# First batch's pairs loaded in rows of 8 tokens per partition, their factors handed over by TensorE with selection matrices; x casts first in a block

## The chip, the cores and the metric

The kernel runs on one core of a Trainium2 chip. Time is device microseconds for one execution. A time quoted for a kernel is the median of several runs; a profile shows one execution in detail, and its span leaves out about two microseconds that lie around it.

The engines are named as the profile names them: PE is TensorE's matmul stream (PEld its weight loads), DVE is VectorE, ACT is ScalarE, POOL is GpSimd, SP is SyncE, which here only issues DMAs. ACT and POOL issue DMAs too.

## The reference, cut to what matters

Two stages. The first is a state-space scan over 4 batches, 8 heads, 768 tokens, head width 32, state width 16, in chunks of 32 tokens:

```python
cum = np.cumsum(np.log(a), axis=-1)                 # within a chunk
L = np.exp(cum[:, :, :, None] - cum[:, :, None, :]) * causal
y_intra = einsum('bhij,bhjd->bhid', (C @ B.T) * L, x)
y_inter = einsum('bhin,bhnd->bhid', C, state) * exp(cum)
state = exp(sum(la)) * state + sum_j(B_j x_j * exp(cum_last - cum_j))
y = y_intra + y_inter
```

The second is a gated feed-forward layer over the 3072 tokens, with the heads laid side by side (256 columns) and a hidden width of 1536:

```python
out = (np.maximum(y @ w_gate, 0) * (y @ w_val)) @ w_out
```

The decay between two tokens is a ratio of running products of `a`. So the kernel multiplies each row of C by the running product at its token (the factor FC) and each row of B by its inverse (FB); the scan then becomes plain matmuls with a causal mask.

## The kernel before, in words

**Tiling.** Work goes in chunks of 128 tokens. Two chunks are a pair (256 tokens); a batch has PPB = 3 pairs, the program 12. A feed-forward block is 512 tokens, two pairs; there are 6 blocks. The 12 slices of 128 hidden columns are counted by f.

**Layout of B and C.** `load_rows` (L75) loads a whole batch of B or C in one DMA: partition q*32 + r holds, for heads q and q + 4 (index t), the 24 consecutive tokens from 24 r on (K = 24), 16 values each. In this layout each partition has a contiguous stretch of tokens, which `factors` (L161) needs for the running product: a scan over 24 tokens in each partition, a 32x32 transpose, a scan over the 32 partitions' totals, a transpose back, a product. The result is FC, [128, 2 per batch, 24].

`scale` (L194) multiplies rows by factors and writes bf16; `turn` (L203) transposes 32x32 blocks of 32-bit words on VectorE, after which the state index lies on the partitions; `tidy_b`, `tidy_c` (L209, L221) put the tokens in order, as BT and CT (CT twice, each with one head of a partition group masked out by `tmask`).

**A pair's attention.** `cast_x` (L239) makes x bf16. `rows_b` (L250) transposes BT on TensorE and copies it (tile bt). `G` (L260) forms the products of C and B into four PSUM banks; `gevac` (L278) brings them to SBUF, two banks through ACT with the causal mask applied by POOL (`causal`), two through DVE with a mask product. `astep` (L298) adds bt times x to the state in PSUM (A_ps), `sevac` (L307) copies it out (Sm); `state` is both. `inter` and `Dm` (L322, L334) form y from the state and from the masked products, `yevac` (L348) copies it to yT.

**The feed-forward part.** `gvh` (L374) does half a block (256 tokens) of one f: gate and val matmuls, Relu on ACT, product on DVE; `gv` (L360) does 512 tokens. `fout` (L390) multiplies by w_out; `foevac` evacuates and stores through SP.

**What sets the order.** Every engine runs its instructions in the order in which the program issues them (`in_order`, L16, adds this as a dependency). There is no planner: the loop over blocks names, for each f, what is interleaved there. In block b the pairs are P = 2b + 2 and Q = 2b + 3, prepared for the next block; W = 2b + 1 is finished in the middle of block b. `scale_new` (L464) scales the next batch, `turn_new` turns it.

**Queues.** SP issues loads of a, B, C, x and the stores; ACT issues the second piece of `a` and the first C; POOL issues the weights (`weights(f0, f1)`, L141, for slices f0 to f1 of gate and val; `weights_out`, L147), which are cast to bf16 on the way. `wait_for` (L154) is a one-element POOL copy that holds POOL's later DMA issues back until a load has landed. `keep_warm` (L130) issues filler matmuls. Shared PSUM tiles (`bank`, L69) rotate over six banks.

**Start.** Lines L416 to L446: factors of batch 0, its C and B scaled, turned and tidied on DVE and ACT, pair 0's attention, the beginning of pair 1's. Then the loop over blocks, whose block 0 finishes pair 1 (gevac(1) at f = 0, L475; state, inter, Dm from L484).

## Time and profile before

| | |
|---|---|
| median of 7 runs | 137.55 us (135.96 to 140.48) |
| the profiled execution | 136.55 us, of it span 134.5 us |
| mean granted TensorE clock | 0.975 |
| PE busy | 119.4 us, 89% of the span |
| DVE busy | 93.4 us, 69% |
| ACT busy | 80.8 us, 60% |
| POOL busy | 44.4 us, 33% |
| DMA | 12.07 MB in 34,701 packets, 26,496 of them under 512 B |

Issue to landing, medians: x loads (128 KB each) 4.9 us; B 3.8 and C 4.3 (384 KB each); gate and val weights (256 KB written each) 5.0 and 5.6; w_out (768 KB written) 10.3.

How to read it: busy shares are averages over stages that have different limits. The chain of waits says, for each moment, which work the end of the program hung on; the busy times by window say which engine had no time left in a stage. Blocks start (first gvh matmul) at 14.1, 37.4, 57.4, 78.2, 96.5 and 114.6 us from the span's start.

### The profile page before, as it was taken

The numbers are of one execution on the slowest core, as the hardware profiler recorded it, in microseconds if no ns is written. First come the engines' busy times: TensorE is split into PE (matmuls) and PEld (weight loads), VectorE is DVE, ScalarE is ACT, GpSimd is POOL, SyncE is SP. The second block draws the span as 40 slices with busy tenths as digits, with TensorE's granted clock in tenths as the row PEclk, the third lists the DMA queues.
The fourth block names the chain that finished last, engine by engine and source line by source line (L and its number), as shares of the span: only waits on it lengthen the run. The fifth ranks groups of instructions, "written<-read, shape, count | busy, mean of one in ns | idle before, by whom it ended". The sixth has DMA issues, their size and how long they took to land.

```text
span 134.5 us, 2889 instructions
## 1 busy us (share of the span) xinstructions
PE 119.4 (89%) x1057; PEld 77.0 (57%) x1057; DVE 93.4 (69%) x210; ACT 80.8 (60%) x177; POOL 44.4 (33%) x75
## 2 busy tenths in 40 slices
PE   6829849799999789999499999999999999999990
PEld 2204526347786347786147786467784477854770
DVE  6676476998588867668556879775686965687510
ACT  4055647564598743598554498954889635876410
POOL 3417355655250951251950270402524012200000
PEclk9975799999999999999999999999999999999999
DMA  2994899990239700239600227200270002200021
GB/s 56 279 173 66 142 222 251 212 190 4 83 92 292 86 0 5 78 113 279 83 0 0 78 80 123 38 2 0 83 156 0 0 5 78 78 5 0 0 101 55
DMA packets 34701, 12.07 MB, mean 90 GB/s; under 512 B 26496, under 2 KB 34688, under 8 KB 34688
## 3 DMA queue, kind: packets, MB, share of 16 engines
q1 hardware_dynamic: 30800, 8.87, 31.2%
q0 software_dynamic: 3184, 2.36, 11.6%
q10 hardware_dynamic: 704, 0.67, 1.5%
q8 instruction: 8, 0.13, 0.4%
q14 instruction: 5, 0.04, 0.1%
HBM read 11.11 MB, written 3.15 MB: 106 GB/s over the span
## 4 chain that ended last, share of the span: by engine, by line
PE 68%; DVE 9%; DMA 7%; issue 5%; POOL 4%; ACT 3%; SPq 1%; ACTq 0%; DVEq 0%; POOLq 0%
PE o L395 22%; PE gv L383 13%; PE gate L365 12%; PE val L368 11%; DMA xr<-in_x_dram 3%; DMA cr<-in_C_dram 3%; DVE h L372 3%; PE g L267 3%; PE y L340 3%; POOL sqB L198 2%; PE A_ps L303 2%; PE y L329 2%; DVE h L387 1%; PE bb L255 1%; POOL gs L274 1%
## 5 line engine op out<-in xcount | busy, mean ns | idle before, releaser
L372 DVE TENSOR_TENSOR h<-r,val 128x512 bf16<-128x512 bf16 x48 | 32.2, 683 | 8.5 <-ACT r L371 7.8
L371 ACT ACTIVATE r<-gate 128x512 bf16<-128x512 f32 x48 | 28.3, 598 | 13.2 <-PE gate L365 10.0
L395 PE MATMUL o<-wo,h 128*128 128x256 bf16 x288 | 34.9, 273 | 0.1
L395 PEld LDWEIGHTS <-h 128*128 128x128 bf16 x288 | 27.4, 98 | 5.2 <-issue 1.3
L365 PE MATMUL gate<-yT,wg 128*128 128x512 bf16 x96 | 28.6, 379 | 0.0
L368 PE MATMUL val<-yT,wv 128*128 128x512 bf16 x96 | 28.6, 379 | 0.0
L274 POOL TENSOR_SCALAR_AFFINE_SELECT gs<-gs 128x512 bf16<-128x512 bf16 (+1 forms) x24 | 12.2, 530 | 44.0 <-ACT gs L285 44.0
L387 DVE TENSOR_TENSOR h<-r,gv 128x256 bf16<-128x256 bf16 x48 | 19.8, 421 | 7.3 <-ACT r L386 6.7
L291 DVE TENSOR_TENSOR gs<-g,maskUT 128x512 bf16<-128x512 f32 x24 | 15.5, 686 | 12.0 <-PE g L267 8.9
L386 ACT ACTIVATE r<-gv 128x256 bf16<-128x256 f32 x48 | 18.4, 386 | 3.3 <-PE gv L383 1.8
L383 PE MATMUL gv<-yT,wg 128*128 128x256 bf16 x96 | 18.8, 278 | 0.9 <-ACT yT L353 0.5
L383 PE MATMUL gv<-yT,wv 128*128 128x256 bf16 x96 | 18.6, 276 | 0.0
L368 PEld LDWEIGHTS <-wv 128*128 128x128 bf16 x96 | 9.4, 98 | 11.4
L365 PEld LDWEIGHTS <-wg 128*128 128x128 bf16 x96 | 9.0, 98 | 11.4 <-issue 4.2
L353 ACT CAST yT<-y 128x512 bf16<-128x512 f32 x12 | 7.0, 585 | 10.0 <-PE y L340 8.5
L285 ACT CAST gs<-g 128x512 bf16<-128x512 f32 x12 | 7.1, 588 | 8.9 <-PE g L267 8.9
L383 PEld LDWEIGHTS <-wg 128*128 128x128 bf16 x96 | 9.0, 99 | 3.2 <-issue 1.6
L311 DVE TENSOR_TENSOR Sm<-A_ps,smask 128x256 bf16<-128x256 f32 x20 | 8.2, 410 | 3.4 <-PE A_ps L303 3.4
L383 PEld LDWEIGHTS <-wv 128*128 128x128 bf16 x96 | 9.5, 99 | 1.3
L227 POOL TENSOR_SCALAR CT<-tqC,tmask 128x264 bf16<-128x264 bf16 (+1 forms) x10 | 9.3, 932 | 0.0
L225 ACT ACTIVATE CT<-tqC,tmask 128x264 bf16<-128x264 bf16 (+1 forms) x13 | 6.7, 526 | 4.2 <-DVE tqC L205 4.2
L198 POOL TENSOR_TENSOR sqC<-cr,FC 128x384 bf16<-128x384 f32 x6 | 5.3, 879 | 11.8 <-DMA cr<-in_C_dram 9.3
(65 smaller groups left out, 105.8 us busy)
## 6 DMA issues: line engine op xcount, KB each, us to landing
xr<-in_x_dram SPq DMA_DIRECT2D x24, 128.0 KB, 4.9
out_dram<-ob SPq DMA_DIRECT2D x10, 256.0 KB, 2.2
br<-in_B_dram SPq DMA_DIRECT2D x4, 384.0 KB, 3.8
cr<-in_C_dram SPq DMA_DIRECT2D x3, 384.0 KB, 4.3
wg<-in_moe_w_gate_dram POOLq DMA_DIRECT2D x3, 256.0 KB, 5.0
wv<-in_moe_w_val_dram POOLq DMA_DIRECT2D x3, 256.0 KB, 5.6
wo<-in_moe_w_out_dram POOLq DMA_DIRECT2D x1, 768.0 KB, 10.3
cr<-in_C_dram ACTq DMA_DIRECT2D x1, 384.0 KB, 4.5
```

Of the source, the lines that this page charges most:

```text
L227: eng.tensor_scalar_mul(dst, src, tmask[:, t:t + 1])
L274: nc.gpsimd.affine_select(out=dst, in_=dst, pattern=[[0, n], [1, 128]], compare_op=ALU.is_ge, fill=0.0, base=0, channel_multiplier=-1)
L291: nc.vector.tensor_tensor(out=d[:, q], in0=g[q], in1=m, op=ALU.mult)
L311: nc.vector.tensor_tensor(out=n, in0=A_ps, in1=smask, op=ALU.mult)
L365: nc.tensor.matmul(out=g, lhsT=wg[:, k, fs], rhs=yT[:, k, tk], start=(k == 0), stop=(k == 1))
L368: nc.tensor.matmul(out=v, lhsT=wv[:, k, fs], rhs=yT[:, k, tk], start=(k == 0), stop=(k == 1))
L371: nc.scalar.activation(r, g, AF.Relu)
L372: nc.vector.tensor_tensor(out=fst[b][:, f], in0=r, in1=v, op=ALU.mult)
L383: nc.tensor.matmul(out=gv_[:, j], lhsT=w[:, k, fs], rhs=yT[:, k, tk], start=(k == 0), stop=(k == 1), skip_group_check=True)
L386: nc.scalar.activation(r, gv_[:, 0], AF.Relu)
L387: nc.vector.tensor_tensor(out=fst[b][:, f, u * 256:(u + 1) * 256], in0=r, in1=gv_[:, 1], op=ALU.mult)
L395: nc.tensor.matmul(out=o[:, ts % 2], lhsT=fst[b][:, f, ts * 128:(ts + 1) * 128], rhs=wo[:, f], start=(f == 0), stop=(f == NF - 1), skip_gr ...
```

## The change

**Batch 0.** B and C of the first batch are no longer loaded as a whole but pair by pair, in a layout of 8 consecutive tokens per partition (K8 = 8): partition q*32 + r holds tokens 256 p + 8 r on. Each pair's B and C take four DMAs each (one for each group q of 32 partitions, 32 KB); pair 0's alternate between ACT and SP, pair 1's follow, pair 2's go out inside block 0.

The factors are still computed in the layout of 24 tokens per partition. `give` brings them into the other layout: token group r of pair p is the s-th third of partition row c with 3c + s = 32p + r, so three FP32 matmuls with 0/1 selection matrices (`hand`, made by POOL in `hands`), each on a third of FC's columns, add up to the pair's factors in PSUM. `take` forms the inverse and, if asked, copies the factors to SBUF. `scale8`, `turn8`, `tidy8_b`, `tidy8_c` are the counterparts of the old functions on 8 tokens per partition. Pairs 1 and 2 are scaled on POOL.

**Start.** `tmask` is built on POOL instead of DVE, bd and smask later on DVE (`more_masks`). Fillers: 14 become 6, then 5 after `give(1)`; the 3 before Dm(0) become 5.

**Weights.** `weights(4, 8)` before block 0 and `weights(8, NF)` at its f = 1 become one `weights(4, NF)` at f = 0, after gevac(1).

**Loads in the blocks.** Block 0's loads go out at f = 0 behind a POOL memset that follows the weights: pair 2's B and C, x(2), batch 1, x(3), x(4), batch 2. Block b > 0 loads the x of pairs P + 1 and P + 2, and then batch b + 2 instead of b + 1.

**Casts first.** In blocks b > 0 POOL casts P and Q at f = 0 and 1 and scales the next batch at f = 2 to 5; before, scaling came at f = 0 to 3 and the casts at f = 4 and 5.

```diff
+    def load_pair(p, j, q, eng):
+        b, c0 = p // PPB, 2 * (p % PPB)
+        src = {"B": B, "C": C}[j][b].rearrange("(t q) s n -> q t s n", t=2)
+        eng.dma_start(
+            out=st[p]["rows"][j][R * q:R * q + R],
+            in_=src[q][:, c0 * 128:(c0 + 2) * 128].rearrange("t (r k) n -> r t (k n)", r=R))
...
-    nc.sync.dma_start(out=al[:, 0:1, 1:], in_=av[:, 0:1])
-    nc.scalar.dma_start(out=al[:, 1:2, 1:], in_=av[:, 1:2])
+    nc.sync.dma_start(out=al[:, 0:2, 1:], in_=av[:, 0:2])
...
-    rows["C", 0] = load_rows(C, 0, nc.scalar, "cr")
-    rows["B", 0] = load_rows(B, 0, nc.sync, "br")
-    load_x(0, nc.sync)
+    for j in "CB":
+        for q in range(4):
+            load_pair(0, j, q, (nc.scalar, nc.sync)[q % 2])
+    load_x(0, nc.sync, nc.scalar)
+    for j, q in (("C", 0), ("C", 1), ("C", 2), ("C", 3), ("B", 0), ("B", 1), ("B", 2), ("B", 3)):
+        load_pair(1, j, q, nc.scalar if j == "C" and q < 2 else nc.sync)
     load_x(1, nc.sync)
...
+    hand = const.tile([128, PPB, 3, 128], FP32)
+
+    def hands(p0, p1, eng):
+        n = p1 - p0
+        eng.memset(hand[:, p0:p1].rearrange("p c s i -> p (c s i)"), 0.0)
+        for q in range(4):
+            h = hand[R * q:R * q + R, p0:p1, :, R * q:R * q + R]
+            nc.gpsimd.affine_select(
+                out=h, in_=h, pattern=[[R, n], [-1, 3], [1, R]], base=R * p0,
+                channel_multiplier=-3, compare_op=ALU.not_equal, fill=1.0)
...
+    hands(0, 1, nc.gpsimd)
     make_identity(nc, ident)
...
+    hands(1, 2, nc.gpsimd)
...
+    def give(p):
+        s = st[p]
+        f = bank("f8", (128, 2, K8))
+        for i in range(3):
+            nc.tensor.matmul(out=f, lhsT=hand[:, p, i], rhs=FC[:, 0:2, K8 * i:K8 * i + K8],
+                             start=(i == 0), stop=(i == 2))
+        s["f"] = {"C": f}
+        return f
+
+    def take(p, keep):
+        s = st[p]
+        f = s["f"]["C"]
+        s["f"]["B"] = fb = const.tile([128, 2, K8], FP32, name="fb%d" % p)
+        if keep:
+            s["f"]["C"] = fc = const.tile([128, 2, K8], FP32, name="fc%d" % p)
+            nc.vector.tensor_copy(fc, f)
+        nc.vector.reciprocal(fb, f)
+
+    def scale8(p, j, eng):
+        s = st[p]
+        s.setdefault("sq", {})[j] = sq_ = att.tile([128, K8 // 2, 2, N, 2], BF16, tag="sq8" + j, name="sq8")
+        for t in range(2):
+            eng.tensor_tensor(
+                out=sq_[:, :, t],
+                in0=s["rows"][j][:, t].rearrange("p (a k n) -> p a n k", n=N, k=2),
+                in1=s["f"][j][:, t].rearrange("p (a k) -> p a k", k=2)
+                .unsqueeze(2).to_broadcast([128, K8 // 2, N, 2]), op=ALU.mult)
...
     factors(0, 2)
+    give(0)
+    give(1)
+    keep_warm(5)
+    more_masks(0)
+    scale8(0, "C", nc.vector)
+    take(0, False)
+    turn8(0, "C")
+    wait_for(0, st[0]["rows"]["B"][96:97, 0, 0:1])
     weights(0, 4)
+    tidy8_c(0, 0, nc.scalar)
+    scale8(0, "B", nc.vector)
+    turn8(0, "B")
+    tidy8_c(0, 1, nc.scalar)
+    tidy8_b(0, nc.vector)
+    take(1, True)
+    more_masks(1)
     cast_x(0, nc.scalar)
+    scale8(1, "C", nc.gpsimd)
+    scale8(1, "B", nc.gpsimd)
...
     gevac(0, half=False)
+    hands(2, 3, nc.gpsimd)
     sevac(0, 0)
+    turn8(1, "C")
+    turn8(1, "B")
+    tidy8_c(1, 0, nc.scalar)
+    tidy8_b(1, nc.vector)
+    tidy8_c(1, 1, nc.vector)
+    keep_warm(5)
     Dm(0)
...
+        def loads():
...
+            if b == 0:
+                load_batch(1)
+            for n in (P + 1, P + 2):
+                if n < NPAIR:
+                    load_x(n, nc.sync)
+            load_batch(b + 2)
...
             if b == 0 and f == 0:
                 gevac(1)
-            if b > 0:
-                scale_new(f)
+                wait_for(1, st[1]["xr"][0:1, 1, 0, 0:1])
+                weights(4, NF)
+                for k in range(8):
+                    if k == 0:
+                        nc.gpsimd.memset(st[2]["rows"]["C"][:, 0, 0:1], 0.0)
+                    load_pair(2, "CB"[k // 4], k % 4, nc.sync)
+                load_x(2, nc.sync)
+                loads()
+                give(2)
+            if b > 0 and more and f < 2:
+                cast_x(P + f, nc.gpsimd)
+            if b > 0 and f >= 2:
+                scale_new(f - 2)
             if b == 0 and f == 1:
                 cast_x(1, nc.scalar)
-                weights(8, NF)
+                take(2, True)
                 wait_for(2, st[2]["xr"][0:1, 1, 0, 0:1])
                 weights_out(0, NF)
-            if b == 0 and f == 3:
+            if b == 0 and f == 2:
                 state(1, 0)
...
             if b == 0 and f == 4:
-                tidy(P, nc.vector, nc.scalar, nc.gpsimd)
-            if b == 0 and f < 8:
-                scale_new(f - 4)
-            if at("cast P", 5, 4, 4):
-                cast_x(P, nc.gpsimd)
-            if at("cast Q", 8, 5, 4):
-                cast_x(Q, nc.gpsimd)
+                scale8(2, "C", nc.gpsimd)
+                scale8(2, "B", nc.gpsimd)
+            if b == 0 and f == 6:
+                turn8(2, "C")
+                turn8(2, "B")
+                tidy8_c(2, 0, nc.scalar)
+                tidy8_c(2, 1, nc.gpsimd)
+                tidy8_b(2, nc.vector)
+            if b == 0 and 5 <= f < 9:
+                scale_new(f - 5)
+            if b == 0 and f in (4, 8):
+                cast_x(P + (f == 8), nc.gpsimd)
+            if b > 0 and f < 6:
+                scale_new(f - 2)
```

## The prediction

> **What bounds the kernel now.** I read the page's busy line first, then the chain of waits in order of time, then busy time by block, then the DMA queues in short windows.
>
> The chain gives the opening. Its columns are start, length, what (us).
>
> ```profile
> 1.23 4.49 DMA cr<-in_C_dram
> 5.74 1.04 DVE sqC L198 x2
> 6.81 0.58 DVE tqC L205
> 7.39 0.92 DVE sqB L198 x2
> 8.33 0.59 DVE tqB L205
> 8.94 0.39 DVE BT L216
> 9.37 0.39 PE bb L255 x2
> ...
> 11.00 1.22 POOL gs L274 x2
> ```
>
> Nothing starts before the whole batch's C has landed (5.72); then five VectorE steps on 768 tokens run in series up to 9.33. GpSimd's causal masks (to 12.2) and TensorE's y lead to the first feed-forward matmul at 14.1.
>
> Busy time by feed-forward block (blocks 1 to 4, bounds at each block's first gv matmul; columns: stretch, length, then busy us and count for PE, PEld, DVE, ACT, POOL, then clock, DMA share, GB/s):
>
> ```profile
> 37.38:57.35 19.97, 18.54 (x175) 12.37 (x174) 15.20 (x32) 12.88 (x30) 8.23 (x13) 1.00 0.41 93
> 57.35:78.20 20.85, 18.62 (x178) 12.58 (x177) 14.53 (x30) 13.39 (x30) 8.66 (x14) 1.00 0.40 89
> 78.20:96.45 18.25, 18.25 (x177) 12.40 (x175) 13.31 (x27) 13.08 (x29) 4.99 (x9) 1.00 0.28 60
> 96.45:114.55 18.10, 18.10 (x175) 12.26 (x173) 13.34 (x28) 12.55 (x28) 4.84 (x8) 1.00 0.19 44
> ```
>
> Blocks 3 and 4 are TensorE without a gap, 18.1 to 18.25. Blocks 1 and 2 are 1.8 and 2.65 longer. The same chain says why, here in block 2:
>
> ```profile
> 59.68 4.59 DMA xr<-in_x_dram
> 64.33 0.88 POOL sqB L198
> ...
> 66.00 0.89 POOL sqB L198
> 66.89 0.57 POOL xb L242
> 67.50 0.27 PE A_ps L303
> ```
>
> GpSimd works in order: its four scalings of the next batch wait for that batch's load (the waits put 4.6 us on C's landing), the casts of x stand behind them, and TensorE's state matmul behind those (TensorE idle 2.2 us before 67.5, 1.4 us before 47.59). VectorE is the limit once, in block 0, from 22 to 32 (8.81 busy of 9.00 between 22 and 31).
>
> In block 0 the DMA engines are also full from 14 to 30. Queue 0 (GpSimd's casting weight loads) and queue 1 (SP's) between 26 and 27 us; columns packets, MB, share of 16 engines:
>
> ```profile
> q0 software_dynamic: 372, 0.19, 138.7%
> q1 hardware_dynamic: 130, 0.02, 20.9%
> ```
>
> The last weight load before wo lands 8.2 us after its issue at 17.77, wo 10.3 us after 20.09, that is at 30.4, when fout first wants it.
>
> **What the Trainium skill says.** "DMA: Bandwidth & Descriptors", section Queues, rings and completion order: each DMA engine goes round-robin over its queues packet by packet. The two lines above agree: against queue 0's packets of about 500 B (0.19 MB in 372), x's 128 B pieces get 0.02 MB in a microsecond; alone, between 7 and 8, they got 0.15. "TensorE: Matmul & The Clock Gate", What's actually happening: the array runs at half rate until it has been busy for about 3.4 us. Agrees: filler matmuls come every 0.43 us until 5.0, every 0.215 later; and the clock is again 0.50 from 9 to 15, after TensorE idled from 6.3 to 9.4. "FP8 and Floating Point Precision", TensorE Precision Notes: true FP32 takes four passes. No FP32 matmul is in this trace.
>
> **The change part by part.**
>
> *Loads at the start.* One 384 KB load of C and one of B become four 32 KB loads each for pair 0, then eight more for pair 1. Issue costs 0.46 us for 256 rows and 1.05 for an x load of 1,024 pieces, so some 0.35 for 64 rows (estimate on that slope). ACT issues seven DMAs, 6 x 0.35 + 1.0 = 3.1: its table load (1.28) then ends near 5.4 instead of 3.0; first use at 6.25, so free. SP's first B row is out by 2.6 and lands near 4.9 (2.0 to landing for a small load, plus queueing); C by 4.3. C stops being what is waited for; FC is: the scan starts when al lands (2.84 now, 0.1 later as one DMA), FC at 4.2.
>
> *The handing over.* Three FP32 matmuls of 16 columns for each pair, not in the trace. Low: three bf16 issues, 0.3 us. High: four passes, each with a 0.13 us weight load at half clock, 3 x 4 x 0.13 = 1.6. I take 1.0: f at 5.2. VectorE's five bd memsets (0.5) move into this wait and cost nothing; if f came at once they would cost 0.5.
>
> *VectorE on 256 tokens instead of 768.* A scale of 384 is 0.53 to 0.56, so 128 is some 0.26; a turn of 384 is 0.57 and of 32 0.21, so 128 is 0.31. C scale 0.5, reciprocal of 16 0.2 (48 take 0.45), turn 0.3, B scale 0.5, turn 0.3, tidy 0.37: 5.2 + 2.2 = 7.4 against 9.33.
>
> *GpSimd at the start.* The selection matrices: a memset of 384 is 0.41 (0.10 for 1, 0.20 for 128), four selects of 96 0.27 each (0.29 for 128): 1.5 a set. First set by 2.3; identity, tmask, triangle 1.7; second set by 5.5. The weight issue moves from 5.48 to 5.7: covered, weights are wanted at 12.5 and land near 12. **give(1)** waits for that second set on TensorE's in-order queue, and five fillers (2.1 cold) and then rows_b(0) stand behind it: bb at 7.5 to 8.2 instead of 9.37. Third set (1.5) after the first masks: idle there.
>
> *Up to block 0.* New on GpSimd ahead of the masks: four scalings of pair 1, 1.44 (0.36 each from 0.88 for 384), from 7.75 to 9.2; masks end at 10.5 instead of 12.2. VectorE gets two turns (0.6) and take(1) (0.3). Following the old intervals, G(1) ends and the first gv starts at 12.5: **1.6 us earlier**.
>
> *Small moves.* Fillers: 14 become 6 at the start (TensorE then waits for FC anyway), 3 become 5 before Dm(0): 2.1 us cold from 8.6 end at 10.7, where Dm waits for the mask at 10.5; I count 0. give(2) (0.3 to 1.6) and take(2) (0.3) come between f=0 and f=1 of block 0; TensorE idles 1.4 us before 18.93 there, waiting for VectorE, so give(2) lies in that gap, and take(2) is the price, paid back by state(1, 0) one f earlier. The output stores of block 0 stand on SP behind batch 2's two loads (1 us of issue); nothing waits for a store there, three ob buffers cover it.
>
> *Weights 4 to 12 in one pair of DMAs.* Half were issued at 12.3; now all go after gevac(1)'s mask, where the second pair went at 17.06: with the 1.6, at 15.4. Flow starts 1.7 later (12.29 to 14.0 now). Alone queue 0 moves 0.20 MB/us (15 to 17); 1.05 MB with SP's loads joining after 18.8 at about 0.15: done 23.4, landed near **24.0**. val of f=4 wants it at 20.8 (22.4 less 1.6): TensorE waits 3.2. VectorE's factors(2, 8) (2.1) run inside that wait.
>
> *x(2) and GpSimd's queue.* SP now issues eight pair-2 loads (2.8 us) ahead of x(2), all behind a GpSimd memset at 17.3, against weights that win the round-robin. I put x(2)'s landing at **24.5** (19.6 before). GpSimd stands at that wait, and wo, pair 2's scalings, the cast, and batch 1's scalings are behind it: 0.17 + 1.03 + 1.44 + 0.62 + 0.88 + 0.9 + 0.88 + 0.88 = 6.8, so batch 1's C can be turned at 31.3. VectorE, in order, has turn, h, turn, Sm, h left: 0.57 + 0.69 + 0.57 + 0.4 + 0.69 = 2.9. The last h is at 34.2 (31.87 before): **2.3 us later than before**. wo, issued at 24.7, flows some 5 us from 26.5: 32, where fout begins; covered.
>
> *Blocks 1 and 2.* Batches load a block earlier and the P cast comes first, of an x loaded a block earlier. The Q cast waits for an x issued at the block's start (landed +5 us), the scalings end at +9.1; TensorE wants P's state at about +8.5 and VectorE the C turn at +8.7 (three scalings, +8.3). All covered, the turn by 0.4. Gain 1.75 + 2.6 = **4.35**. Blocks 3 to 5 unchanged: TensorE has no gap to give.
>
> Sum on the profiled execution (span 134.5, time 136.55): +2.3 - 4.35 = -2.0, 134.5. The median of the runs is 137.55, 1.0 above it, spread 3.3%; I carry the difference over: **135.5**.
>
> **The rivals.**
>
> A, likeliest (0.50): as summed, -2.0, own range -3.5 to -0.5, so 134.0 to 137.0: x(2)'s landing is known to 1.5 us.
>
> B (0.24): the loads are not late. For it: with less requested by SP, weights run at 0.20 throughout, landing at 22. Then VectorE's 8.5 us (eight h 5.5, turns of pair 2 0.6, of batch 1 1.14, tidy 0.4, Sm 0.8) bound block 0: fout's first group 1.0 early, -1.0 - 4.35: 132.2. Against it: GpSimd still waits for x(2).
>
> C, slower (0.20): x(2) starves behind the weights. For it: queue 1's 0.02 MB between 26 and 27; at that rate x(2) lands only after the weights, the eight pair loads and itself: 24 + 0.7 + 1.8 + 2 = 28.5. Everything behind GpSimd's wait moves with it: 4.0 later, +2.0: 139.6. It breaks even at a landing of 26.5 and is slower by 1% from 27.9. Against it: 18.8 to 24 leaves SP's queue some of the engines (between 22 and 24 it had about half).
>
> D (0.06): the hand-over fails as a short cut: 1.6 us for give and selects at twice my price hold give(1) and its fillers to 9.5, the start gains nothing, and the delay passes to the weights' issue: 1.6 later, -0.4: 137.1. Against it: the select rows.
>
> **How the numbers follow.** About 1% (1.4 us) is what can be told from no change. Faster by over 1%: A 0.33, B 0.24: 0.57. Within: A 0.15, C 0.01, D 0.04: 0.20. Slower: A 0.02, C 0.19, D 0.02: 0.23. The range 131.8 to 139.2 leaves out a third of B below (0.08) and half of C above (0.11).
>
> **What would show it.** C's scale at 5.2 with FC before it, bb near 7.9, first gv at 12.5; TensorE idle at val of f=4 until 24; GpSimd's gate copy of x(2) at 24.5 and VectorE waiting for GpSimd's sqC near 31; no TensorE wait on xb in blocks 1 and 2, each near 18.3. It is wrong if that gate copy comes before 22 or after 26.5, if give takes over 1.6, or if the Q cast's landing now holds the scalings and the turn.

## The result, and the profile after

The changed kernel takes **138.41 us** (median of 12 runs, 137.34 to 143.12) where the kernel before takes 136.91 (31 runs, 135.96 to 140.48): the ratio is **1.0095, interval 1.0057 to 1.0132**. A gain of 2 us was forecast; it lost 1.5. Its profiled execution took 137.93 us with a span of 136.2 us. In what follows a ratio is always to the kernel before, run beside it on the same chip. In some of the runs below the profiled execution, or most of the timed ones, fell into a slower state of the chip: no time is read from such a trace, and no ratio stands where none could be formed.

Busy time by block, first of the kernel before (the opening and block 0), then of the changed one (the opening, then blocks 0 to 3); the columns are those of the prediction's block view, stretch, length, the five engines, clock, DMA share, GB/s.

```profile
0.00:14.11 14.11, 9.63 (x57) 3.51 (x58) 9.39 (x40) 5.65 (x11) 5.70 (x17) 0.80 0.79 138
14.11:37.38 23.27, 19.93 (x179) 12.69 (x176) 17.58 (x40) 13.66 (x31) 11.48 (x17) 0.98 0.94 159
```

```profile
0.00:13.80 13.80, 11.74 (x69) 5.83 (x69) 7.61 (x38) 5.51 (x11) 10.47 (x37) 1.00 0.72 121
13.80:43.35 29.55, 22.11 (x182) 13.29 (x181) 18.54 (x44) 14.33 (x32) 13.49 (x25) 0.94 0.84 162
43.35:61.83 18.48, 18.45 (x176) 12.37 (x174) 14.90 (x32) 12.87 (x30) 8.26 (x13) 1.00 0.40 100
61.83:80.11 18.28, 18.28 (x176) 12.43 (x174) 14.16 (x30) 13.24 (x30) 8.50 (x13) 1.00 0.28 59
80.11:98.35 18.24, 18.24 (x177) 12.39 (x174) 13.23 (x28) 13.06 (x30) 4.98 (x9) 1.00 0.28 59
```

Read the lengths. Blocks 1 and 2 are now 18.48 and 18.28, TensorE busy for all but 0.03 us of them: they were 19.97 and 20.85, so the late part of the change brought its 4.1 us. The opening is 0.3 shorter. **Block 0 is 29.55 instead of 23.27**, 6.3 longer, and TensorE's busy time in it grew by only 2.2: the rest is waiting. The clock column doesn't tell all: it gives 1.00 for the opening, but the fillers below come 0.43 us apart (five in 2.13 us), half the rate that the prediction read for fillers later on (0.215), so TensorE was cold there.

The opening, in the chain of waits of the changed kernel (start, length, what):

```profile
6.19 1.46 PE f L226 x6
7.66 2.13 PE w L169 x5
9.79 0.21 PE bb L339 x2
10.00 0.65 PE g L351 x8
```

The f line is pair 1's handing over, three FP32 matmuls (six records); the w line the five fillers behind it. B could be read at 7.73 (9.31 before), but bb comes at 9.58 where it came at 9.37. On GpSimd, the scaling of pair 1 and the masks (timeline; in brackets the idle time before the instruction and what ended it):

```profile
8.06 0.85 POOL L244 TENSOR_TENSOR sq<-r8C,fc 128x128 bf16<-128x128 f32 x2
10.16 0.79 POOL L244 TENSOR_TENSOR sq<-r8B,fb 128x128 bf16<-128x128 f32 x2 [1.25 <-DMA r8B<-in_B_dram]
11.23 1.22 POOL L358 TENSOR_SCALAR_AFFINE_SELECT gs<-gs 128x512 bf16<-128x512 bf16 x2 [0.29 <-ACT gs L369]
```

Two holds of nearly equal length lie here. On TensorE the fillers push bb and G back, and the masks, which GpSimd applies to G once ACT has copied it, could start at 11.23: that copy is what ended the 0.29 us before them. On GpSimd the last of pair 1's B rows landed at 9.9, so the scalings that stand ahead of the masks ended at 10.95, only 0.3 earlier. Taking one hold away leaves the other.

Block 0, again in the chain:

```profile
17.24 0.71 POOL wv L180
17.95 0.11 POOL r8C L581
18.07 10.41 issue
28.52 0.09 POOL gate L191
28.62 8.00 DMA wo<-in_moe_w_out_dram
36.66 1.37 PE o L479 x11
```

From the last weight issue at 17.24 the chain goes to the memset that lets SP's loads go (L581), then 10.41 us in which GpSimd only waits, then the one-element gate copy, wo's issue and its 8.00 us, then the output. The output of block 0 begins at 36.66 (30.42 before). What the 10.41 us wait for is in the timeline of GpSimd, and in SP's own waits up to 40 us (line, what for, us in total, times, longest):

```profile
28.50 0.17 POOL L191 COPY gate<-xr 1x1 f32<-1x1 f32 x1 [10.43 <-DMA xr<-in_x_dram]
```

```profile
SPq L99 <- POOL r8C L581: 7.4, 1, 7.4
SPq L87 <- DMA r8C<-in_C_dram: 2.1, 3, 1.3
```

x(2), which goes in two halves, has landed at 28.4. SP stood 7.4 us at the memset; then it issued eight loads of pair 2 (18.09 to 22.97), and x(2)'s first half only at 24.26, when pair 2's first load had landed, 6.1 us after its issue; the second half went at 24.96, when pair 2's second load had landed. In the same time the DMA queues moved (20 to 22 us; packets, MB, share of 16 engines), first in the changed kernel, then in the one before:

```profile
q0 software_dynamic: 208, 0.40, 109.1%
q1 hardware_dynamic: 12, 0.01, 1.5%
```

```profile
q0 software_dynamic: 244, 0.23, 74.0%
q1 hardware_dynamic: 157, 0.24, 36.1%
```

Pair 2's C loads were waiting on queue 1 and got 0.01 MB of 0.41 against the merged weights; in the kernel before SP's loads had half of the bytes. That half is an average of two unlike microseconds: 17 of 188 packets from 20 to 21 (5.7% of the engines), 140 of 213 from 21 to 22 (66.6%). TensorE meanwhile waits 1.6 us for the gate weights and 2.3 for the value weights, which land at 25.7.

### The profile page after: what moved, and what is told of

It reads as the page before. It is cut to its first block, busy times and chain, and to the rows that moved or that the text cites. A ratio compares the mean times of both kernels' runs of the same rounds, so it can differ in the third digit from the quotient of the medians.

```text
span 136.2 us, 3001 instructions
## 1 busy us (share of the span) xinstructions
PE 123.4 (91%) x1074; PEld 79.8 (59%) x1074; DVE 92.0 (68%) x212; ACT 81.3 (60%) x177; POOL 51.2 (38%) x102
## 3 DMA queue, kind: packets, MB, share of 16 engines
q1 hardware_dynamic: 31056, 8.95, 28.9%
## 4 chain that ended last, share of the span: by engine, by line
PE 74%; issue 9%; DMA 6%; POOL 5%; ACT 1%; DVE 1%; POOLq 0%; DVEq 0%; ACTq 0%
PE o L479 24%; PE gv L467 14%; PE gate L449 13%; PE val L452 13%; DMA wo<-in_moe_w_out_dram 6%; PE g L351 3%; PE y L424 2%; PE w L169 2%; PE A_ps L387 1%; POOL hand L138 1%; PE y L413 1%; PE f L226 1%; PE bb L339 1%; POOL gs L358 1%; DVE gs L375 1%
## 5 line engine op out<-in xcount | busy, mean ns | idle before, releaser
L452 PE MATMUL val<-yT,wv 128*128 128x512 bf16 x96 | 29.5, 390 | 2.3 <-DMA wv<-in_moe_w_val_dram 2.3
L449 PE MATMUL gate<-yT,wg 128*128 128x512 bf16 x96 | 29.4, 389 | 1.6 <-DMA wg<-in_moe_w_gate_dram 1.6
L479 PEld LDWEIGHTS <-h 128*128 128x128 bf16 x288 | 27.3, 98 | 5.2 <-issue 1.3
L467 PE MATMUL gv<-yT,wv 128*128 128x256 bf16 x96 | 18.3, 273 | 0.0
L326 POOL CAST xb<-xr 128x512 bf16<-128x512 f32 x10 | 6.1, 610 | 13.6 <-DMA xr<-in_x_dram 6.8
L311 POOL TENSOR_SCALAR CT<-tqC,tmask 128x264 bf16<-128x264 bf16 (+1 forms) x9 | 8.4, 933 | 0.0
L169 PE MATMUL w<-warm 128*128 128x512 bf16 x16 | 6.9, 595 | 1.3 <-DVE warm L122 1.3
```

What stands on the lines that cost most here:

```text
L169: nc.tensor.matmul(out=w, lhsT=warm[:, 0:128], rhs=warm, start=True, stop=True)
L311: eng.tensor_scalar_mul(dst, src, tmask[:, t:t + 1])
L449: nc.tensor.matmul(out=g, lhsT=wg[:, k, fs], rhs=yT[:, k, tk], start=(k == 0), stop=(k == 1))
L452: nc.tensor.matmul(out=v, lhsT=wv[:, k, fs], rhs=yT[:, k, tk], start=(k == 0), stop=(k == 1))
L467: nc.tensor.matmul(out=gv_[:, j], lhsT=w[:, k, fs], rhs=yT[:, k, tk], start=(k == 0), stop=(k == 1), skip_group_check=True)
L479: nc.tensor.matmul(out=o[:, ts % 2], lhsT=fst[b][:, f, ts * 128:(ts + 1) * 128], rhs=wo[:, f], start=(f == 0), stop=(f == NF - 1), skip_gr ...
```

## The experiments

The theory after this trace: block 0 is lost to what its loads do to each other, above all x(2), which GpSimd waits for. Rivals were x(2)'s place on SP, wo's gate, the size of the weights' pieces, the weights' late start, the number of small loads, and the opening. Output of block 0 below is the start of its first o matmul.

### The late part by itself, and the opening

**The kernel before with the batches a block earlier and the casts first**

```
+        load_batch(b + 2)
...
+            if b > 0 and more and f < 2:
+                cast_x(P + f, nc.gpsimd)
```

> The kernel before with only the late part of the change: batches loaded a block ahead, and in blocks b > 0 the casts of x at f = 0 and 1 with the scalings of the next batch at f = 2 to 5. Theory (the late part gains what blocks 1 and 2 lost, the rest of the change costs): blocks 1 and 2 last 18.3 to 18.5 instead of 20.0 and 20.85, the start and block 0 stay as in the kernel before, 3.7 to 4.4 us faster than the kernel before, ratio near 0.97. Rival (blocks 1 and 2 are only clean in the changed kernel because block 0 ended 6 us later, which gave their loads time): no more than 1.5 us gained. Second rival (batch 2's loads, now in block 0's full DMA queues, make block 0 later): blocks 1 and 2 clean, block 0 longer by 1 us or more.

Measured: 132.62 us, ratio 0.9652 (0.958 to 0.9725). Its blocks 1 and 2:

```profile
37.54:56.01 18.47, 18.39 (x174) 12.39 (x173) 14.88 (x32) 12.88 (x30) 8.23 (x13) 1.00 0.41 100
56.01:74.40 18.39, 18.34 (x176) 12.54 (x175) 14.26 (x30) 13.36 (x30) 8.61 (x14) 1.00 0.28 58
```

The same lengths as in the changed kernel, with the old opening (first feed-forward matmul, gv, at 13.98; output of block 0 at 30.53). So the late part is worth 3.5% by itself, and all that the changed kernel loses against this run, some 6 us, is lost before block 1.

**Fillers taken out** (the changed kernel without `keep_warm(5)` behind give(1))

```
     give(1)
-    keep_warm(5)
```

> The changed kernel without the five filler matmuls between give(1) and rows_b(0). Theory (the start's gain of 1.6 us on VectorE was taken back on TensorE's in-order queue, where give(1) ends at 7.65 and the fillers at 9.78 at 0.43 us each): bb starts near 7.8 instead of 9.58, the first gv near 12.2 instead of 13.8, the weights go out 1.5 us earlier and the whole kernel is 1.0 to 1.7 us faster than the changed one (about the time of the kernel before). Rival (the start is bounded by pair 1's loads and scalings, or by GpSimd's masks behind them): bb moves, the first gv does not, under 0.5 us gained. Second rival (the fillers keep the clock up): the clock stays at half for longer and the gain is eaten there.

Measured: ratio 1.0128 (1.0031 to 1.0225). bb came at 7.49, 2.1 earlier, and the first gv at 13.64, 0.16 earlier. GpSimd:

```profile
10.29 0.79 POOL L244 TENSOR_TENSOR sq<-r8B,fb 128x128 bf16<-128x128 f32 x2 [1.30 <-DVE Sm L395]
11.03 1.25 POOL L358 TENSOR_SCALAR_AFFINE_SELECT gs<-gs 128x512 bf16<-128x512 bf16 x2
```

The fillers covered the second hold: the masks, now straight behind pair 1's scaling, come only 0.2 us earlier than with them. (The releaser named is VectorE's Sm, which ended at 10.10; the last of B's loads was issued at 7.0 and the slowest took 3.1 us, so the rows were there no earlier.)

**Masks first as well** (`scale8(1, ...)` moved behind `gevac(0)`)

> The changed kernel without the five fillers and with GpSimd's scalings of pair 1 moved behind gevac(0)'s masks. Theory (the start has two holds, the fillers on TensorE and pair 1's scalings, waiting for their B rows until 10.2, ahead of the masks on GpSimd; taking one away shows nothing, as the run without fillers did, taking both away shows the gain): masks end near 10 instead of 12.4, yT of pair 0 is there by 11.5 instead of 13.7, the first gv starts at 12.6 to 13.0 instead of 13.8, held then by pair 1's own turn, tidy and G. The whole gains 0.5 to 1.2 us if the later DMA work moves with it, nothing if it does not. Rival (pair 1's B rows hold G(1) and with it the first gv as they are): first gv stays at 13.5 or later.

Measured: ratio 1.0103 (0.9995 to 1.0212), no better. That block 0 sets the output and takes up what the opening wins would explain it; no trace of this run shows it.

### One thing at a time in block 0

**x(2) ahead of pair 2's loads, still behind the memset**

```
+                load_x(2, nc.sync, after=nc.gpsimd)
                 for k in range(8):
...
-                load_x(2, nc.sync)
```

> The changed kernel with x(2) issued on SP ahead of pair 2's eight loads, behind the same weights. Theory (GpSimd's wait for x(2), held up by eight loads that SP can only issue slowly beside the weights, sets when wo is issued and so when fout begins): x(2) lands 3 to 5 us earlier than 28.5, wo is issued as much earlier and fout of block 0 begins near 33 instead of 36.7, the kernel is 2.5 to 4 us faster than the changed one. Rival (the late gate and val weights, 22.8 and 25.7, and the half clock after that stall bound block 0 by themselves): fout begins no earlier than 35.5, gain under 1.2 us. Second rival (x(2)'s 128 B pieces starve as badly beside the weights as the pair loads did): x(2) lands after 26.5 all the same, gain under 1.5 us.

Measured: ratio 1.0427 (1.0322 to 1.0532). x(2), issued at 18.64, landed at 27.3, 8.7 us later; the loads behind it were held back still more, batch 1's C was squared only at 36.25, output at 40.90. As long as all of SP's loads start behind the weights, another order on SP doesn't help.

**wo not gated by x(2)**

```
-                wait_for(2, st[2]["xr"][0:1, 1, 0, 0:1])
```

> The changed kernel without the one-element GpSimd copy that waits for x(2): wo is issued right behind the gate and val weights, near 18. Theory (that wait is what makes fout late): wo lands before 32, fout begins when VectorE's last h is there, 34 or earlier, 2.5 us or more faster than the changed kernel, although x(2) and pair 2's rows land later. Rival (the loads of x(2), pair 2 and batch 1 are what block 0 really needs, and wo ahead of them only moves the stall to GpSimd's scalings and VectorE's turns): wo is early, but the last h comes no earlier than 36, gain under 1 us.

Measured: ratio 1.0335 (1.0252 to 1.0417). wo went out at 18.35 and landed at 30.6; batch 1's C then waited in its place:

```profile
34.26 0.88 POOL L282 TENSOR_TENSOR sqC<-cr,FC 128x384 bf16<-128x384 f32 x1 [1.66 <-DMA cr<-in_C_dram]
```

The gate protects SP's loads from wo; without it the stall moves on.

**The weights in two pairs, back to back** (`weights(4, 8)`, `weights(8, NF)` at the same place)

> The changed kernel with weights(4, NF) issued as weights(4, 8) and weights(8, NF), one directly behind the other at the same place. Theory P (size of the pieces: queue 0 moves 4 to 12 in pieces of about 2 KB and so leaves SP's 512 B and 128 B pieces nothing until it is done): pieces halve to 1 KB, SP's queue moves at least twice as many packets between 21 and 24 as the 12 to 66 per us of the changed kernel, x(2) lands 1.5 us or more earlier, val of f=4 (25.7) starts near 22.5, and the kernel is 1 us or more faster than the changed one. Theory Q (the casting loads take the engines whatever their pieces are; what counts is when they start, 4 us later than in the kernel before): val of f=4 starts earlier, x(2) lands within 1 us of 28.5, fout begins at 36 to 37, the whole within 1 us of the changed kernel.

Measured: ratio 1.0161 (1.0045 to 1.0277). The first gate weights came earlier (21.99 instead of 22.84), but queue 1 still got 0 to 50 packets in each microsecond until 24, x(2) landed at 28.6, output at 38.80. Smaller pieces without a gap between them gave SP little here. The test isn't a clean one: pair 2's loads stood behind four weight issues instead of two and went out only from 20.03 (18.09 in the changed kernel), so they had less time on the queue.

**The weights earlier** (`weights(4, NF)` right behind `hands(2, 3)`)

> The changed kernel with wait_for(1) and weights(4, NF) moved up to directly behind hands(2, 3), ahead of gevac(1)'s masks on GpSimd. Theory Q (block 0 is bounded by one unbroken run of DMA work that starts when these weights are issued and ends when wo lands; it starts 4 us later than before): the DMA engines fill about 2 us earlier (near 16 instead of 18), everything up to wo's landing comes 1.5 to 2.2 us earlier, fout near 34.7, the kernel 1.3 to 2.2 us faster than the changed one. Rival (x(2)'s own issue, still behind the GpSimd memset and eight pair loads, keeps its place near 24 on SP): val of f=4 comes earlier, x(2) and wo do not, under 0.7 us gained.

Measured: ratio 1.0054 (1.0018 to 1.009). The weights went out 1.7 us earlier (second one at 15.59 instead of 17.24), but x(2) only at 23.78 and it landed at 27.4, output at 38.00. Here another wait shows. From 24 to 25 queue 0 was empty and queue 1 used 11% of the engines, so nothing starved x(2) by then: it had only just been issued. (The output came later than in the changed kernel, 38.00 against 36.66, though the weights went earlier; this execution's opening was later too, first gv at 14.35.) SP's queue in this run (start, length, line, tile, number):

```profile
17.39 1.80 SPq L99 DMA_DIRECT2D r8C<-in_C_dram  x4
19.24 1.85 SPq L99 DMA_DIRECT2D r8B<-in_B_dram  x4
23.78 1.01 SPq L87 DMA_DIRECT2D xr<-in_x_dram  x2
```

Between 21.09 and 23.78 SP stood at x(2) until pair 2's first C load, issued 6.4 us before, had landed. That load is eight before x(2). The same distance was seen in the changed kernel (18.09 to 24.26) and without wo's gate (18.46 to 25.00). In the traces the DMAs of SP and ACT signal their landings on eight semaphores in turn, and a DMA goes out only when the eighth before it has landed; with a pair in eight loads, one pair fills that row.

**The old order of loads** (weights(4, 8), x(2) and pair 2 before block 0, weights(8, NF) in it, all behind the old gates)

> The changed kernel with the start of e7 and the load order of block 0 as in the kernel before: weights(4, 8) and x(2) directly behind pair 1's scalings, then pair 2's loads without the memset, weights(8, NF) behind gevac(1), the third selection set behind those and give(2) and take(2) after the second halves of f = 0 to 3. Theory Q: the DMA engines fill again from 13 to 14, x(2) lands near 20, wo is issued by 21 and lands by 31, fout begins near 30.5 to 31.5, and with the late part's gain the kernel takes 131.5 to 133.5, like the late part alone (132.6) or up to 1 us better. Rival (pair-wise loading itself, its 24 small loads and the hand-over, costs block 0 its time): fout no earlier than 33.5, 135 or more.

Measured: 140.66 us (four runs, 136.19 to 142.23), no ratio. It settles nothing: the forecast order is neither shown nor refuted.

### Several things together

**SP's loads not held by the memset**

```
-                    if k == 0:
-                        nc.gpsimd.memset(st[2]["rows"]["C"][:, 0, 0:1], 0.0)
```

> The changed kernel without GpSimd's memset that holds block 0's loads on SP (pair 2, x(2), batch 1 and on) until the weights have been issued at 17.95: they go out from about 11, into the stretch 13.2 to 17.8 in which the DMA engines idle. Theory (block 0 loses because these loads are held back until the weights flow, are starved by them, and then find the eight landings short): x(2) has landed before 19, its gate copy stands right behind the weights' issue, wo is issued by 20, output of block 0 begins at 33 to 34.5 instead of 36.7, and the kernel is 2 to 3.5 us faster than the changed one (134.9 to 136.4 against 138.4). Rival (block 0 needs more bytes than its time can move, in any order): batch 1's C loads starve behind weights and wo, as with wo ungated; VectorE's or GpSimd's square of batch 1's C waits past 33, output begins at 36.5 or later, gain under 1 us.

Measured: 137.42 us (four runs, 135.7 to 139.13; the kernel before beside it 137.9), no ratio; span 134.3 against 136.2. Output at 34.44, 2.2 earlier. The theory's way was wrong: of x(2)'s halves, issued at 15.09 and 15.56, the first landed at 17.6 and the second at 25.1 and not before 19, behind the weights that had gone out meanwhile. And only about half of the 2.2 belongs to the edit. The opening of this execution, which the edit doesn't touch, was 1.2 us shorter than the changed kernel's:

```profile
8.87 0.78 POOL L244 TENSOR_TENSOR sq<-r8B,fb 128x128 bf16<-128x128 f32 x2
9.61 1.21 POOL L358 TENSOR_SCALAR_AFFINE_SELECT gs<-gs 128x512 bf16<-128x512 bf16 x2
12.62 0.38 PE L467 MATMUL gv<-yT,wg 128*128 128x256 bf16 x2
```

Pair 1's last B rows happened to land at 8.6 instead of 9.9, and TensorE was warm, so that the five fillers took 1.24 us instead of 2.29. From first gv to output are 21.8 us, against 22.9 in the changed kernel: 1.0 for the edit. By the same luck this trace shows the opening with both holds gone: first gv at 12.62, where 12.5 was forecast.

**The weights earlier besides**

> As the run without the memset, and wait_for(1) with weights(4, NF) moved ahead to behind hands(2, 3), so that the weights go out at about 14.8 instead of 16.5. Theory (weights and SP's loads each come late, and the idle stretch takes both): value weights land by 24 instead of 25.7, TensorE's wait at value f = 4 falls from 2.3-2.8 to under 1 us, output of block 0 begins 1 to 2 us earlier than without the memset alone; time 133.5 to 135. Rival: the weights starve the SP loads again (x(2) lands after 24 or batch 1's C after 32), no better than without the memset alone.

Measured: 135.94 us, ratio 0.9869 (0.9777 to 0.996); output at 33.50. The value weights landed at 24.1 as expected, but TensorE's wait for them was still 2.35; x(2) landed at 25.3.

**The start mended** (fillers out, masks first, weights earlier, no memset)

> The changed kernel with all that the runs point to at its start: the five fillers out, GpSimd's masks of gevac(0) ahead of its scaling of pair 1, the weights issued earlier, and no memset ahead of block 0's loads. Theory (the loss lies in these places and none is of the pairs' layout itself): first gv at 13.5 or earlier, output of block 0 begins at 31.5 to 33, 132 to 134, faster than the kernel before. Rival (24 loads of 32 KB in the layout of 8 tokens per partition cost by themselves, in issue time and landings): output begins after 34, 135 or more, no more than 1 us better than the run with loads and weights moved.

Measured: 134.91 us, ratio 0.9845 (0.9759 to 0.993); first gv 13.11 (13.85 and 13.80 in the two runs below that keep these edits), output at 33.27. The run before it, without the two edits to the opening, has a ratio that can't be told from this one. Between theory and rival: better than both kernels, 2.7 behind the old block 0 (30.53 in the late part alone). What was left there:

```profile
24.62 0.17 POOL L191 COPY gate<-xr 1x1 f32<-1x1 f32 x1 [8.00 <-DMA xr<-in_x_dram]
24.74 1.02 POOL L184 DMA_DIRECT2D wo<-in_moe_w_out_dram  x1
```

**x(2) first in the mended start**, ahead of pair 2's loads

> The mended start (fillers out, masks first, weights earlier, no memset), and besides x(2) on SP ahead of pair 2's eight loads instead of behind them. Left to explain is that there x(2), issued at 15.31, landed only at 24.6 and wo at 33.2, with output of block 0 at 33.27 against 30.53 in the kernel with the later part alone. Theory (what is left of block 0's loss is x(2)'s place on SP: behind eight small loads it meets the weights, ahead of them it does not): x(2) issued by 11 and landed by 15, its gate copy waits for nothing, wo issued at 16.5 to 18 and landed by 29, output of block 0 begins at 30.5 to 31.5; 131.5 to 133, about 2 us better than with x(2) behind. Rival (the small loads and the eight landings only pass the stall on): wo's early transfer starves batch 1's B and C, whose squares begin after 31.5; output begins at 33 or later, no better than 134.5.

Measured: 135.13 us, ratio 0.9814 (0.9776 to 0.9852). The rival was right: x(2) had landed by 16.7 and was there when GpSimd asked, wo went out at 17.03, and again batch 1's C stood in x(2)'s place:

```profile
28.68 0.88 POOL L282 TENSOR_TENSOR sqC<-cr,FC 128x384 bf16<-128x384 f32 x1 [2.35 <-DMA cr<-in_C_dram]
```

Output at 33.28, where it was.

**x(2) first in the changed kernel, without the memset**, nothing else

> The changed kernel without the memset ahead of block 0's loads, x(2) ahead of pair 2's loads; fillers, masks and the weights' place as in the changed kernel. It tells how much of block 0's loss is SP's order and gate alone. Theory (nearly all of it): x(2) landed before its gate copy's turn, wo issued at 17.5 to 19, output of block 0 begins at 31.5 to 33 instead of 36.66; 133 to 135. Rival (the value weights, landing at about 25, hold TensorE in any case and set the output): output begins at 34 or later, as with the memset alone taken out (34.44).

Measured: ratio 1.0079 (1.0022 to 1.0137). wo at 18.41, but the value weights, now sharing with x(2), pair 2 and wo, landed at 27.4, and output began at 36.50. In the changed kernel SP's order and gate alone give nothing.

**Half as many loads** (each pair's B or C in 2 loads of 64 KB over 128 partitions, in the mended start)

```
-        src = ...rearrange("(t q) s n -> q t s n", t=2)
-            out=st[p]["rows"][j][R * q:R * q + R],
+        src = ...rearrange("(t q) s n -> t q s n", t=2)
+            out=st[p]["rows"][j][:, q],
```

> The mended start (fillers out, masks first, weights earlier, no memset; x(2) behind pair 2's loads), with each pair's B or C in 2 loads of 64 KB (one for each head group, all 128 partitions) instead of 4 of 32 KB: 12 loads instead of 24, the same 512-byte rows. Up to 10 us the changed kernel and its mended forms moved 101 to 105 GB/s where the kernel before moved 170, and by 18 us 2.2 MB where it had moved 2.7. Theory (what is left of block 0's loss is the slow issue of small loads, about 0.46 us for 32 KB, and the landings that they use up): 120 GB/s or more up to 10 us, 2.4 MB or more by 18 us, x(2) issued by 13 instead of 15.3, output of block 0 begins at 30.8 to 32.3 instead of 33.27; 132 to 134. Rival (the short rows set the rate, not the number of issues): still 110 GB/s or less up to 10 us, x(2) lands after 23 again, output begins at 33 or later, 134.5 or more.

Measured: ratio 0.9857 (0.9762 to 0.9952), as the mended start. The first 10 us, of the kernel before, of the mended start, and of this run:

```profile
0.00:10.00 10.00, 5.65 (x24) 2.00 (x24) 6.72 (x34) 3.12 (x6) 2.90 (x11) 0.92 0.94 170
```

```profile
0.00:10.00 10.00, 6.90 (x33) 3.20 (x34) 6.12 (x33) 4.37 (x8) 7.48 (x29) 0.88 0.56 102
```

```profile
0.00:10.00 10.00, 7.17 (x30) 3.98 (x31) 5.87 (x32) 3.95 (x8) 6.45 (x28) 1.00 0.49 98
```

The last two columns: 98 GB/s at an engine share of 0.49, against 102 at 0.56 and 170 at 0.94. GB/s divided by share are not far apart (181, 182, 200), so most of the missing rate is time in which the engines moved nothing. Halving the number of loads did not fill it. The rival's outcome came true (98 GB/s, output at 33.78, no faster), but its reason, short rows, would have to show as fewer GB/s at the same share, and accounts for a tenth at most. What keeps the engines idle there is open.

The same edit in the changed kernel:

> The changed kernel with that one edit: pairs in 12 loads of 64 KB instead of 24 of 32 KB; fillers, masks, weights, memset and SP's order as in the changed kernel. Theory (with 4 loads of pair 2 instead of 8 ahead of it, x(2) finds a landing free and is out sooner): x(2) issued by 21.5 instead of 24.26, its gate copy at 25 to 27 instead of 28.50, output of block 0 begins at 34 to 35.8 instead of 36.66; 136 to 137.5. Rival (x(2) is starved by the weights until about 25.5 whenever it is issued, and its landing hardly moves): gate copy at 27.5 or later, output at 36 or later, no better than the changed kernel by 0.8 us.

Measured: ratio 1.017 (1.0125 to 1.0216), no better than the changed kernel (1.0095, interval 1.0057 to 1.0132). It was not followed up.

**The weights in two pairs with the masks between them, in the mended start**

```
-    weights(4, NF)
+    weights(4, 8)
...
+                weights(8, NF)
                 take(2, True)
                 wait_for(2, st[2]["xr"][0:1, 1, 0, 0:1])
```

> The mended start (fillers out, masks first, weights earlier, no memset; x(2) behind pair 2's loads) with the weights 4 to 12 in two pairs of DMAs as in the kernel before: weights(4, 8) at 14, weights(8, NF) at f = 1 of block 0, behind GpSimd's second pair of masks, at about 16.5 to 17. In the kernel before x(2) lands between the two pairs, 5.8 us after its issue. Theory (what is left is that 1 MB of weights in one run shuts SP's queue out until it is through, and x(2), issued at 15.3, can't land before 24.6): in two pairs x(2) lands by 22, wo is issued by 22.5 and landed by 31.5, value f = 4 waits less than 1 us, output of block 0 begins at 30.8 to 32 instead of 33.27; 132.5 to 134. Rival (the second pair follows too closely, or the bytes are late in any order): x(2) lands after 23.5, output at 33 or later, within 0.8 us of the mended start.

Measured: ratio 0.9772 (0.9673 to 0.9872); better than the mended start, though the intervals overlap.

**And x(2) first**

> As the weights in two, and x(2) on SP ahead of pair 2's loads. Theory (in two pairs the weights leave SP's queue room for x(2) and then for pair 2 and batch 1): wo issued by 19, batch 1's C squared from 27 or earlier, output of block 0 begins at 30.5 to 32; 132 to 134. Rival (wo, sent early, shuts out pair 2 and batch 1 as in the run with x(2) first before): batch 1's C is squared at 28.5 or later, output begins at 33 or later, 134.5 or more.

Measured: **133.52 us, ratio 0.9693 (0.9636 to 0.9749)**. wo at 18.70, output at 32.05; the value weights of f = 4 are waited for no more. The queues from 20 to 22 us, first in the run with x(2) first and the weights in one, then in this one:

```profile
q0 software_dynamic: 173, 0.35, 93.1%
q1 hardware_dynamic: 141, 0.06, 16.4%
```

```profile
q1 hardware_dynamic: 252, 0.38, 57.1%
q0 software_dynamic: 175, 0.16, 51.0%
```

Against the run with x(2) first and the weights in one (0.9814) this is the one edit that differs; the intervals do not touch. x(2) had landed before the weights in both. What gets through with the gap is pair 2, whose B rows had landed by 20.9 instead of 24.8, and behind it batch 1's C, squared at 26.46 instead of 28.68; by 20 us queue 1 carries mostly batch 1 (issued from 17.60; 1.5 KB a packet). The edit makes the gap and also halves the weights' pieces. For the gap speaks a look inside this run: with the first half of the weights moving (17 to 18 us) queue 1 got 23 packets against 198, in the gap (19 to 20) 315 against 127. Smaller pieces alone were tried only in the unclean test above, so they aren't ruled out as a part of it.

**The late part alone with x(2) ungated**

> The kernel before with the change's later part alone (batches a block ahead, x casts first), and besides x(2)'s load without GpSimd's memset ahead of it, so that it follows on SP's queue at once. Theory (an early load into an unfilled queue costs nothing and lets wo out earlier): x(2) lands before 15, wo issued at 17 to 18 and landed before 28, so block 0's output begins up to 1 us earlier than in the late part alone (30.53); 131 to 132.6 against its 132.62. Rival: x(2)'s 0.25 MB takes its share from x(1) and the first weights, the first gv comes later than 13.98 by 0.5 or more, and the time is 132.6 to 133.5.

Measured: 132.98 us, ratio 0.9668 (0.9613 to 0.9724), the same as with the gate. wo went out at 17.79 instead of 19.90 and landed at 28.5, but the output began at 31.05, no earlier than with the gate; the rival's later gv did not come either (13.73). Where x(2) isn't late, bringing it forward is worth nothing.

| kernel | first gv | weights issued (last) | x(2) gate copy | wo issued | batch 1's C first squared | output | ratio |
|---|---|---|---|---|---|---|---|
| before | 14.11 | 17.77 | 19.65 | 20.09 | 24.61 | 30.42 | 1 |
| changed | 13.80 | 17.24 | 28.50 | 28.62 | 31.72 | 36.66 | 1.0095 |
| memset out | 12.62 | 16.18 | 25.12 | 25.24 | 28.34 | 34.44 | none |
| and weights earlier | 13.94 | 15.08 | 25.33 | 25.45 | 28.55 | 33.50 | 0.9869 |
| and fillers out, masks first | 13.11 | 14.89 | 24.62 | 24.74 | 27.84 | 33.27 | 0.9845 |
| and x(2) first | 13.85 | 15.24 | 16.91 | 17.03 | 28.68 | 33.28 | 0.9814 |
| and weights in two | 13.80 | 17.87 | 18.58 | 18.70 | 26.46 | 32.05 | 0.9693 |
| late part alone | 13.98 | 17.63 | 19.45 | 19.90 | 24.74 | 30.53 | 0.9652 |

Down to the last but one, each row keeps the edits of the row above; "fillers out, masks first" adds two. 4.6 of the 6.2 us come back. Each time is of one execution, and openings differ by more than a microsecond between executions (first gv), so a single step of less than that isn't to be read; the ratios are firmer. From first gv to output the rows give 16.3, 22.9, 21.8, 19.6, 20.2, 19.4, 18.3 and, for the late part alone, 16.6. No single edit did it: x(2) first behind the weights and wo without its gate passed the stall to batch 1's C, the others tried alone brought nothing that their ratios show. The 1.5 us of output by which the fully mended change still trails the late part alone goes with batch 1's C (squared at 26.46 against 24.74); it was not followed further. The two fastest, the late part alone and the fully mended change, have overlapping intervals: **the pair-wise start, mended, shows no gain** over the old one.

## Why the prediction was wrong

**Block 0: the step that failed.** "I put x(2)'s landing at **24.5**" was 4 us too early: it landed at 28.4, and all that the prediction hung behind GpSimd's wait came those 4 us later (batch 1's C was fully scaled at 35.2). With it fell "covered" for wo: issued at 28.62 instead of 24.7 and 8.0 us on its way, it set the output itself. Block 0 was forecast 2.3 us late; its output was 6.2 late. This term by itself turns the forecast into a loss: -2.0 + 3.9 is +1.9, and the span grew by 1.7. The prediction had named the sign, a gate copy after 26.5; it came at 28.50.

Three things were mis-sized within it. First, the issue: eight loads at 0.35 us were to be out in 2.8; they took 4.9 (18.09 to 22.97). Some 0.46 went to each (the four B loads took 1.85), 1.7 to the second C load alone, for a reason that the profile doesn't name. Then the wait for the eighth landing before it, which the prediction did not know, held x(2) for another 1.3, to 24.26.

Second, the share: the prediction argued from the kernel before that SP would have "about half" of the engines between 22 and 24; it had 12% from 22 to 24 and 1.5% from 20 to 22. The evidence against "about half" lay in the kernel before. The stretch from 15 to 17, read there as queue 0 "alone", had x(2) waiting on queue 1, issued at 13.83 and 14.24; from 16 to 17 it got this:

```profile
q0 software_dynamic: 198, 0.20, 119.2%
q1 hardware_dynamic: 46, 0.01, 4.1%
```

In the next microsecond, when the first weights were all but through (26 packets of queue 0), queue 1 moved 1,511 packets: x(2) came through in a gap that the change removed. The sentence of the Trainium skill on which the share rested ("DMA: Bandwidth & Descriptors", Queues, rings and completion order: round-robin packet by packet) fits only some stretches of these runs: with x(2) first, 293 packets of queue 0 against 291 of queue 1 from 24 to 26; with the weights in two besides, 679 against 680 from 26 to 28. It does not fit the prediction's own two lines (372 against 130), nor the 198 against 46 here, nor the changed kernel's 208 against 12 while loads waited on queue 1. Here the measurement decides; why queue 1 got so little is open. (The counts are sums over 16 engines, and the profile doesn't say which engine took which packet, so the two queues may have met on a few of them only.)

Third, merging the weights was priced only at TensorE's wait, 3.2 us (measured 1.6 + 2.3), with VectorE's work inside it. Its other price was the lost gap: taken back last, with x(2) already first, it was worth 1.2% by the two ratios (0.9814 to 0.9693), smaller pieces included.

**Rival C** named this mechanism and its landing, 28.5, and gave 139.6: 1.2 above the measured 138.4, about half of it because the kernel before has a median of 136.91 over more runs and not 137.55. It was held at 0.20 because of the "about half" above. That 28.5 meets 28.4 so closely is in part luck: C had x(2) waiting on its queue until weights done at 24 let it through, while the weights landed at 25.7 and x(2)'s halves were not even issued until 24.26 and 24.96.

**The start.** 1.6 us were forecast, 0.3 came. The handing over took 1.43 us for pair 0 on a cold TensorE, within the bounds (0.3 to 1.6) and above the 1.0 taken; f was at 5.86 instead of 5.2. The upper bound came from the four passes that the Trainium skill gives for FP32 ("FP8 and Floating Point Precision", TensorE Precision Notes); 1.43 lies a little under it, and the trace, with two records for each of the three matmuls, doesn't show the passes. In executions with TensorE warm the same three took 0.8 to 0.9. Two terms failed, each hiding the other. The fillers behind give(1) put bb at 9.58 where 7.5 to 8.2 was forecast (rival D's "fillers to 9.5"), so that the masks could start only at 11.23. And "four scalings of pair 1 ... from 7.75 to 9.2" took pair 1's B as landed; the last landed at 9.9, and the scalings ended at 10.95. The masks ended at 12.4 instead of 10.5. Where both holds were gone, the first gv came at 12.62.

**The late part.** Right in mechanism and size: 4.1 of the 4.35, in the changed kernel and by itself. The Q cast and the turns stayed covered.

**Weights.** Issued at 16.5 and 17.2 instead of 15.4, by what the start had lost; landed at 22.8 (gate) and 25.7 (value) instead of 24.0.

## What to carry to other kernels

Cost a load that moves behind others by what it finds there: the queue's share against the traffic of that very stretch, and how many landings it may have open, not by its bytes. Two transfers with a gap between them are not the same as one of twice the size, since the gap is where the other queue's urgent load gets through. When several loads compete in one stretch, undoing one edit at a time can show nothing, since one stall hides or hands on to another: add the edits up, and take the part that needs none of it (here the batches loaded a block earlier) by itself.

## What the runs showed of the hardware

- A load on SP waited for the landing of the eighth load before it on SP and ACT in three kernels (6.2, 6.4 and 6.5 us from that load's issue). The traces show why: the DMAs of these two engines signal on eight semaphores in turn. It is a property of how this program counts its landings, and it makes small loads dear: eight of 32 KB use up what eight of 384 KB do.
- Loads of 32 KB were issued 0.46 to 0.50 us apart, about as far apart as the 384 KB loads of 256 rows, and pair 0's eight landed 1.9 to 2.4 us after their issue in the opening, pair 1's up to 3.0. The Trainium skill ("DMA: Bandwidth & Descriptors", Anatomy of one DMA) gives a fixed cost of about 2.0 us on GpSimd's path; these, on SP's and ACT's, come close to it.
- Against 1 MB of casting weights issued together SP's queue, with rows of 512 B waiting, got 12 packets of 220 in 2 us; against the same weights in two parts, with rows of 1.5 KB waiting, it got 252 of 427. Later in that second kernel (26 to 28 us) the two queues went one for one, 680 packets against 679. What sets the share is open.
- After waiting 1.6 us for the gate weights and 2.3 us for the value weights TensorE ran at half clock for 3.2 us (matmuls 0.43 us apart from 25.7 to 28.9).
